# Softmax of a windowed attention: the maximum as a bias and the sum from ScalarE's accumulator, in eight calls per tile

## The chip, the cores and the metric

The kernel runs on one core of a Trainium2 chip. The metric is the device time of one execution in microseconds. The core has five engines with a queue of their own each: TensorE (PE: matmuls, with PEld for its weight loads), VectorE (DVE), ScalarE (ACT), GpSimd (POOL) and SyncE (SP), whose queue issues the DMAs here. An engine works through its queue in program order, and one engine waits for another by semaphores.

## The reference

Three stages follow one another, all in float32. First a chunked attention with 4 batches, 8 heads, 768 positions and a head size of 64: each chunk of 32 queries sees 8 memory keys, 16 keys to the left, its own 32 and 8 to the right, 64 keys in all.

```
scores = scale * matmul(q_c, k_full.T)
scores = scores - max(scores, axis=-1)
a = exp(scores)
a = a / (sum(a, axis=-1) + 1e-09)
out[chunk] = matmul(a, v_full)
```

Its output is laid out as 3072 tokens of 512 numbers. Then comes a gated layer, `(sigmoid(x @ w_gate) * (x @ w_val)) @ w_out` with 1536 inner columns, and a second layer, `silu(x @ w_in) @ w_out` with 2048 inner columns. Some weights come in as 8-byte floats.

## The kernel before, in words

**Attention tiles.** The attention is cut into 24 tiles of 128 tokens. A tile has, on each of the 128 partitions, eight groups of 64 scores: 512 columns, one PSUM bank. Four functions handle a tile, each a step of its own:
- `att_scores` (L181): 16 calls that write the scores into PSUM (L189), with masked columns at a sequence's ends (L197, L199), then on VectorE the maximum of each group (L202) and the subtraction that moves the scores to SBUF (L203), then on ScalarE one Exp over all 512 columns (L204).
- `att_norm` (L207): VectorE's sum of each group (L210), an addition of 1e-9 (L211), the reciprocal (L212) and the multiplication (L213).
- `att_turn` (L215): four transposes on TensorE (L219) and ScalarE's copy out of PSUM (L220).
- `att_pv` (L223): the product with v (L229) and VectorE's transpose into the x tile (L236).

**Opening.** Tiles 0 to 3 run before anything else (the loop at L386): in each turn the scores of tile i, the turn of tile i-2, the norm of tile i-1 and the product of tile i-3. Idle matmuls (L375) stand between them. The x tile is then split into a high and a low part (`split`, L79: ScalarE casts the high part at L82, VectorE or GpSimd computes the low part at L85), which gives each product three matmuls.

**Phase 1.** Six blocks of 512 tokens follow, each with 12 steps f. A step has the gate product into one PSUM bank (`pg`, L263), ScalarE's Sigmoid of it (L273), the value product into another bank (`pv`, L263), VectorE's multiplication of the two (L277), the split of the result g, and the output product of the step before (`y`, L90 to L94). The banks of `pg` and `pv` come from a ring of two: the next step's `pg` waits for the Sigmoid, the next `pv` for L277.

During block 0 a `Feed` brings in the weights. Each of its 36 units is loaded, scaled by ScalarE (`rebias`, L107), put together by three VectorE instructions (`join`, L115, L118, L122), and split into high and low parts (L82 on ScalarE, L85 on GpSimd). During blocks 1 to 5 a generator (`prepare2`) does much the same with the second layer's weights, with sums of them (L478) and with splits that are written to DRAM (`coi`, `coo`).

**Order around the change.** The whole order is written by hand. The attention of tiles 4 to 23 is spread over blocks 0 to 4, four tiles per block, by a table of events, at three places per step f:

```
at = 3 * NF1 * bi + 3 + 24 * jj // max(n - 1, 1)
for d, what in ((0, "scores"), (2, "norm"), (4, "turn"), (6, "pv")):
```

At each place the events come first, and then a step of the `Feed` (block 0) or of the generator (two places in three of the later blocks). So in ScalarE's queue the Exp of a tile stands ahead of that step's casts and rebias, and of the cast of g or of the next Sigmoid. In VectorE's queue the softmax steps stand ahead of a join and of L277. Exp and Sigmoid need different activation tables on ScalarE, so a table load stands ahead of the Exp and another ahead of the next Sigmoid.

**Phase 2.** The second layer (pairs of inner columns, L658, and its output product, L771) uses no attention code.

Of the kernel before, what the change touches and what calls it, by code (L numbers as in the profile page):

```python
# [8 lines left out]
F32 = mybir.dt.float32  # L9
F32R = mybir.dt.float32r  # L10
I32 = mybir.dt.int32
AF = mybir.ActivationFunctionType
ALU = mybir.AluOpType
AX = mybir.AxisListType

P = 128
B, H, S, D = 4, 8, 768, 64
CH, LEFT, RIGHT, NMEM = 32, 16, 8, 8
WIN = NMEM + LEFT + CH + RIGHT
# [7 lines left out]
SCALE = 1.0 / float(D) ** 0.5  # L27
# [20 lines left out]
def moe_kernel(ctx: ExitStack, tc: tile.TileContext, qh, kh, vh, wg, wv, wo, w2i, w2o, out):  # L48
    nc = tc.nc
# [106 lines left out]
            self.n += 1  # L156


    q_t, k_t, v_t, e_t, at_t, x32 = {}, {}, {}, {}, {}, {}

    def att_load_qk(t, qb, kt):
        nc.sync.dma_start(out=qb.rearrange("p g u q -> p (g u q)"), in_=qh[t])
# [18 lines left out]
    def att_scores(t, ps_sc, e):  # L181
        sc = ps_sc(f"sc{t}")
        scv = sc.rearrange("p (c2 a k) -> p c2 a k", c2=2, a=4)
        qb, kt = q_t.pop(t), k_t.pop(t)
        for c2 in range(2):
            for a in range(4):
                for cp in range(2):
                    c = 2 * c2 + cp
                    nc.tensor.matmul(  # L189
                        scv[cp * 64 : cp * 64 + 64, c2, a],  # L190
                        qb[:, 4 * a + c].rearrange("p u q -> p (u q)"),
                        kt[:, a, c],
                        start=True,
                        stop=True,
                    )
        if t % TPB == 0:
            nc.vector.memset(scv[0:64, 0, :, NMEM : NMEM + LEFT], NEG)  # L197
        if t % TPB == TPB - 1:
            nc.vector.memset(scv[64:128, 1, :, WIN - RIGHT : WIN], NEG)  # L199
        s3 = sc.rearrange("p (g k) -> p g k", k=WIN)  # L200
        m = att.tile([P, 8, 1], F32, tag="m", name=f"m{t}", bufs=2)
        nc.vector.tensor_reduce(m, s3, axis=AX.X, op=ALU.max)  # L202
        nc.vector.tensor_tensor(out=e, in0=s3, in1=m.to_broadcast([P, 8, WIN]), op=ALU.subtract)  # L203
        nc.scalar.activation(out=e, in_=e, func=AF.Exp, scale=SCALE)  # L204
        e_t[t] = e

    def att_norm(t, eng=nc.vector):  # L207
        e = e_t[t]
        r = att.tile([P, 8, 1], F32, tag="r", name=f"r{t}", bufs=2)
        nc.vector.tensor_reduce(r, e, axis=AX.X, op=ALU.add)  # L210
        nc.vector.tensor_scalar_add(r, r, 1e-9)  # L211
        nc.vector.reciprocal(r, r)  # L212
        eng.tensor_tensor(out=e, in0=e, in1=r.to_broadcast([P, 8, WIN]), op=ALU.mult)  # L213
# [69 lines left out]
    with tc.manual_schedule():  # L283
# [5 lines left out]
        att = att_cm.__enter__()  # L289
# [96 lines left out]
        for i in range(n0 + 2):  # L386
            if i < n0:
                att_scores(i, ps_y, es[i])
                idle(NI)
            if 0 <= i - 2 < n0:  # L390
                at = hold[0].tile([P, 512], F32, tag="sg", name=f"at{i - 2}", bufs=3)
                att_turn(i - 2, ps_a, at.rearrange("p (a b q) -> p a b q", a=2, b=2))
                idle(NI if i < 4 else 0)
            if 0 <= i - 1 < n0:
                att_norm(i - 1, nc.gpsimd if i - 1 in NQ else nc.vector)
            if 0 <= i - 3:
                att_pv(i - 3, ps_y, x32[0], (i - 3) * P)
                idle(NI if i < 4 else 0)
            if i == 1:
                prefetch(n0)  # L400
            if i == 4:
                prefetch_v(n0)
            if i == n0:
                units[0].rebias()
                units[0].join()
            if i == n0 + 1:
                units[0].part()
                units[1].rebias()
# [10 lines left out]
        for bi in range(NB1 - 1):  # L419
            n = BLOCKS1[bi + 1] // P  # L420
            for jj in range(n):
                t = starts1[bi + 1] // P + jj
# [4 lines left out]
        def run_events(i):  # L427
            for what, t, bn, jj in events.get(i, []):
                if what == "scores":
                    att_scores(t, ps_a, e_tile(t))  # L430
                    prefetch(t + 1)
                elif what == "norm":
                    att_norm(t)
                elif what == "turn":
                    att_turn(t, ps_a, at_tile(t))
                else:
                    if bn not in x32:
                        x32[bn] = x32_tile(f"x32_{bn}")
                    att_pv(t, ps_a, x32[bn], jj * P)
                    prefetch_v(t + 1)  # L440
# [498 lines left out]
```

## Time and profile before

| | |
|---|---|
| time of the runs, median of 3 | 1166.77 us (1166.34 to 1167.43) |
| the profiled execution | 1165.85 us |
| its span in the profile | 1164.1 us |
| busy: TensorE | 1138.2 us (98%) |
| busy: VectorE | 695.6 us (60%) |
| busy: ScalarE | 487.4 us (42%) |
| busy: GpSimd | 124.5 us (11%) |
| data moved | 248.51 MB, 213 GB/s on average |

The span runs from the first to the last recorded instruction; the execution's time has 1.75 us more around it. Busy shares are averages over stages that differ: phase 1 with the attention lies in roughly the first 700 us, phase 2 behind it. In the rows further down, a line such as L204 is a line of the kernel, `out<-in` are the program's names for tiles, and a time in square brackets, or behind the bar, is the idle time of the engine just ahead of the instruction, with what ended it.

### The profile page before, as it was taken

Reading aid. Unit: us, or ns where it says so; the run is one execution under the profiler, and the core shown is the slowest. Engines: PE = TensorE matmul, PEld = TensorE weight load, DVE = VectorE, ACT = ScalarE, POOL = GpSimd, SP = SyncE. Lnnn points to the kernel's source line nnn. Section 1 sums busy time; section 2 is a strip of 40 time slices with the busy share of each in tenths; the row PEclk is TensorE's granted clock in tenths of the full one; section 3 lists DMA queues with packets and bytes.
Section 4 is the critical chain, followed back from the end, with each engine's and each line's share of the span. In section 5 each row is a group of like instructions: output and inputs, shape, how many; then the busy total and the mean of one; then the engine's idle time right before and its main releaser. Section 6 shows DMA issues by size and latency. Waiting matters only on the chain.

```text
span 1164.1 us, 16020 instructions
## 1 busy us (share of the span) xinstructions
PE 1138.2 (98%) x6319; PEld 927.7 (80%) x6319; DVE 695.6 (60%) x965; ACT 487.4 (42%) x708; POOL 124.5 (11%) x94
## 2 busy tenths in 40 slices
PE   8889999999999999999999999999999999999998
PEld 7667777888888888888887888888888888888887
DVE  7999965455555554554564534347944369634665
ACT  3555544334434433443343224445434454344442
POOL 2545530000000000000000001111001110011000
PEclk9999999999999999999999999999999999999999
DMA  9777767667656666766565356566655575655552
GB/s 314 244 238 246 242 218 238 208 206 227 224 194 212 219 227 194 242 213 203 199 205 211 120 188 199 190 239 237 228 199 192 205 282 215 227 193 203 208 204 86
DMA packets 79210, 248.51 MB, mean 213 GB/s; under 512 B 7584, under 2 KB 23968, under 8 KB 69920
## 3 DMA queue, kind: packets, MB, share of 16 engines
q1 hardware_dynamic: 79136, 247.49, 62.4%
q8 instruction: 50, 0.82, 0.3%
q14 instruction: 24, 0.20, 0.0%
HBM read 199.23 MB, written 48.23 MB: 213 GB/s over the span
## 4 chain that ended last, share of the span: by engine, by line
PE 83%; DVE 12%; DMA 3%; issue 1%; ACT 0%; SPq 0%; DVEq 0%; ACTq 0%
PE o L771 20%; PE c L658 20%; PE pv L263 13%; PE pg L263 13%; PE y L90 5%; PE y L92 5%; PE y L94 5%; PE sc L189 1%; PE px L229 1%; DVE t_wg L122 1%; DVE t_wo L122 1%; DVE t_wv L122 1%; DVE stg_wv L118 1%; DVE stg_wo L118 1%; DVE stg_wg L118 1%; DMA v<-in_vh_dram 1%
## 5 line engine op out<-in xcount | busy, mean ns | idle before, releaser
L658 PE MATMUL c<-xp,wr 128*128 128x512 f32 x1008 | 229.1, 389 | 0.0
L771 PE MATMUL o<-gf,wr 128*128 128x512 f32 x1008 | 229.0, 389 | 0.0
L263 PE MATMUL pv<-x,w 128*128 128x512 f32 x864 | 216.1, 400 | 13.0 <-DVE sg L277 11.4
L658 PEld LDWEIGHTS c<-xp,wr 128*128 128x128 f32 x1008 | 189.2, 188 | 39.3
L771 PEld LDWEIGHTS o<-gf,wr 128*128 128x128 f32 x1008 | 189.2, 188 | 39.3
L263 PE MATMUL pg<-x,w 128*128 128x512 f32 x864 | 210.6, 392 | 1.6 <-POOL x L85 0.9
L263 PEld LDWEIGHTS pv<-x,w 128*128 128x128 f32 x864 | 162.9, 191 | 51.9 <-issue 14.3
L263 PEld LDWEIGHTS pg<-x,w 128*128 128x128 f32 x864 | 160.4, 188 | 38.2 <-ACT x L82 1.5
L85 DVE TENSOR_TENSOR gf<-g,gf 128x1024 fp32r<-128x1024 f32 x84 | 103.8, 1239 | 49.9 <-ACT gf L82 49.6
L82 ACT CAST gf<-g 128x1024 fp32r<-128x1024 f32 x84 | 88.1, 1053 | 86.9 <-PE o L771 73.3
L678 POOL TENSOR_TENSOR s<-s,s 128x512 f32<-128x512 f32 x24 | 35.9, 1497 | 820.7 <-ACT s L677 820.7
L82 ACT CAST g<-sg 128x512 fp32r<-128x512 f32 x72 | 44.7, 621 | 156.8 <-DVE sg L277 156.8
L273 ACT ACTIVATE sg<-pg 128x512 f32<-128x512 f32 x72 | 42.9, 596 | 74.8 <-PE pg L263 61.7
L630 DVE TENSOR_TENSOR s<-c,s 128x512 f32<-128x512 f32 x48 | 33.2, 691 | 65.1 <-PE c L658 63.1
L90 PE MATMUL y<-g,wor 128*128 128x512 f32 x240 | 66.3, 397 | 0.6 <-DVE y L532 0.6
L85 DVE TENSOR_TENSOR g<-sg,g 128x512 fp32r<-128x512 f32 x60 | 41.5, 692 | 41.7 <-ACT g L82 41.7
L92 PE MATMUL y<-g,wor 128*128 128x512 f32 x240 | 64.3, 390 | 0.0
L94 PE MATMUL y<-g,wor 128*128 128x512 f32 x240 | 64.2, 389 | 0.0
L277 DVE TENSOR_TENSOR sg<-pv,sg 128x512 f32<-128x512 f32 x72 | 49.3, 684 | 21.3 <-PE pv L263 21.2
L633 DVE TENSOR_TENSOR g<-g,g 128x1024 f32<-128x1024 f32 x48 | 58.4, 1216 | 0.0
L636 ACT ACTIVATE g<-s 128x512 f32<-128x512 f32 x48 | 30.3, 632 | 54.1 <-DVE s L630 54.1
L92 PEld LDWEIGHTS y<-g,wor 128*128 128x128 f32 x240 | 45.1, 188 | 9.6
(120 smaller groups left out, 1127.3 us busy)
## 6 DMA issues: line engine op xcount, KB each, us to landing
wr<-w2o_d SPq DMA_DIRECT2D x42, 1024.0 KB, 4.8
wor<-wo_d SPq DMA_DIRECT2D x60, 512.0 KB, 4.7
wr<-w2i_d SPq DMA_DIRECT2D x24, 1024.0 KB, 5.0
wr<-w2i_d SPq DMA_DIRECT2D x24, 768.0 KB, 4.4
w2o_d<-coo SPq DMA_DIRECT2D x56, 256.0 KB, 2.8
w2i_d<-coi SPq DMA_DIRECT2D x24, 512.0 KB, 3.0
qA<-in_qh_dram SPq DMA_DIRECT2D x21, 512.0 KB, 4.9
k<-in_kh_dram SPq DMA_DIRECT2D x21, 512.0 KB, 5.5
```

What stands on the lines that cost most here:

```text
L82: nc.scalar.copy(hi, src)
L85: lo_eng.tensor_tensor(out=lo, in0=src, in1=hi.bitcast(F32), op=ALU.subtract)
L90: nc.tensor.matmul(o, w_hi, x_hi, start=first, stop=False)
L92: nc.tensor.matmul(o, w_hi, x_lo, start=False, stop=False)
L94: nc.tensor.matmul(o, w_lo, x_hi, start=False, stop=last)
L263: nc.tensor.matmul(o[:, :n], w[:, pw, kt * P : (kt + 1) * P], x[kt][:, px, :n], start=i == 0, stop=i == len(steps) - 1,)
L273: nc.scalar.activation(out=sg[:, :n], in_=psg[:, :n], func=AF.Sigmoid)
L277: nc.vector.tensor_tensor(out=sg[:, :n], in0=psv[:, :n], in1=sg[:, :n], op=ALU.mult)
L633: nc.vector.tensor_tensor(out=o, in0=a, in1=b_, op=ALU.subtract)
L658: nc.tensor.matmul(o, w[:, pw, i % 4, kt * P : (kt + 1) * P], X[i][:, px, kt], start=first and j == 0, stop=j == 5, skip_group_check=not f ...
L678: nc.gpsimd.tensor_tensor(out=s5, in0=s5, in1=s1, op=ALU.add)
L771: nc.tensor.matmul(c[at[i], dp], w[:, pw, pl, dp * P : (dp + 1) * P], f[:, px, pl], start=i in (A11, S1, S2) and pp == 0 and j == 0, stop= ...
```

## The change

`att_scores` no longer subtracts. The maxima are multiplied by -SCALE on VectorE (128 x 8 numbers), and ScalarE computes the Exp straight from PSUM in eight calls, one for each group of 64 columns. Each call takes the group's scaled maximum as its bias, one number per partition, and the sum of its outputs goes to a column of `r` by the accumulator output. `att_norm` takes `r` as it is and leaves the sum out. Nothing else is changed: no tile is bigger, and no DMA, no event and no order of the steps is another.

```diff
-    q_t, k_t, v_t, e_t, at_t, x32 = {}, {}, {}, {}, {}, {}
+    q_t, k_t, v_t, e_t, r_t, at_t, x32 = {}, {}, {}, {}, {}, {}, {}
...
         nc.vector.tensor_reduce(m, s3, axis=AX.X, op=ALU.max)
-        nc.vector.tensor_tensor(out=e, in0=s3, in1=m.to_broadcast([P, 8, WIN]), op=ALU.subtract)
-        nc.scalar.activation(out=e, in_=e, func=AF.Exp, scale=SCALE)
-        e_t[t] = e
+        nc.vector.tensor_scalar(out=m, in0=m, scalar1=-SCALE, scalar2=None, op0=ALU.mult)
+
+        r = att.tile([P, 8, 1], F32, tag="r", name=f"r{t}", bufs=2)
+        for g in range(8):
+            nc.scalar.activation(
+                out=e[:, g], in_=s3[:, g], func=AF.Exp, scale=SCALE, bias=m[:, g], accum_out=r[:, g]
+            )
+        e_t[t], r_t[t] = e, r
 
     def att_norm(t, eng=nc.vector):
-        e = e_t[t]
-        r = att.tile([P, 8, 1], F32, tag="r", name=f"r{t}", bufs=2)
-        nc.vector.tensor_reduce(r, e, axis=AX.X, op=ALU.add)
+        e, r = e_t[t], r_t.pop(t)
         nc.vector.tensor_scalar_add(r, r, 1e-9)
```

## Rows read from the trace of the kernel before

**Rows 1.** The page, parts 1 and 2: busy times, and 40 slices in tenths.

```profile
PE 1138.2 (98%) x6319; PEld 927.7 (80%) x6319; DVE 695.6 (60%) x965; ACT 487.4 (42%) x708; POOL 124.5 (11%) x94
...
PE   8889999999999999999999999999999999999998
...
DVE  7999965455555554554564534347944369634665
```

**Rows 2.** Busy time by stretch: PE, PEld, DVE, ACT, POOL, clock, DMA share, GB/s.

```profile
28.00:150.00 122.00, 106.97 (x627) 81.95 (x626) 114.50 (x140) 66.65 (x106) 65.60 (x44) 0.96 0.74 242
262.00:374.00 112.00, 112.00 (x715) 91.01 (x714) 62.57 (x113) 44.12 (x68) 0.00 (x0) 1.00 0.67 220
```

**Rows 3.** Chain that ended last, 0 to 160 us: start, us, what.

```profile
20.53 5.91 DMA stg_wv<-in_wv_dram
...
28.97 1.45 DVE stg_wv L115
...
156.11 1.61 DVE t_wo L122
```

**Rows 4.** Groups by line and shape: count | busy us, mean ns | idle before.

```profile
L82 ACT CAST g<-sg 128x512 fp32r<-128x512 f32 x72 | 44.7, 621 | 156.8 <-DVE sg L277 156.8
L273 ACT ACTIVATE sg<-pg 128x512 f32<-128x512 f32 x72 | 42.9, 596 | 74.8 <-PE pg L263 61.7 <-DMA yd<-y 9.6 <-DVE y L532 2.3
L203 DVE TENSOR_TENSOR e<-sc,m 128x512 f32<-128x512 f32 x21 | 14.5, 691 | 0.7
L210 DVE TENSOR_REDUCE r<-e 128x8 f32<-128x512 f32 x21 | 14.2, 677 | 0.0
L204 ACT ACTIVATE e<-e 128x512 f32<-128x512 f32 x21 | 13.3, 633 | 37.0 <-DVE e L203 36.9
L211 DVE TENSOR_SCALAR r<-r 128x8 f32<-128x8 f32 x24 | 4.1, 171 | 0.8
L82 ACT CAST coo<-fo 128x256 fp32r<-128x256 f32 x8 | 3.2, 404 | 19.6 <-DMA w2o_d<-coo 19.6
```

**Rows 5.** Timeline of the opening: start, us, engine, line [idle before].

```profile
7.88 0.69 DVE L202 TENSOR_REDUCE m<-sc 128x8 f32<-128x512 f32 x1
...
19.38 0.60 PE L219 MATMUL pt<-ident,e_w 128*128 128x128 f32 x4
...
19.91 1.08 PE L229 MATMUL px<-v,at 128*32 128x128 f32 x32
20.02 0.58 ACT L220 COPY at<-pt 128x512 f32<-128x512 f32 x1 [1.62 <-PE pt L219]
...
25.42 0.65 PE L229 MATMUL px<-v,at 128*32 128x128 f32 x16 [0.70 <-DMA v<-in_vh_dram]
...
26.12 0.72 DVE L236 STREAM_TRANSPOSE x<-px 128x512 f32<-128x512 f32 x1 [0.54 <-PE px L229]
...
27.04 2.17 ACT L82 CAST x<-x 128x512 fp32r<-128x512 f32 x4
```

**Rows 6.** Timeline of block 0 around tile 5.

```profile
75.34 1.28 ACT L204 ACT_TABLE_LOAD   x1
...
76.64 0.63 ACT L204 ACTIVATE e<-e 128x512 f32<-128x512 f32 x1
...
77.68 0.67 ACT L107 ACTIVATE stg_wv<-stg_wv 128x512 f32<-128x512 f32 x1
...
80.14 0.69 DVE L118 SCALAR_TENSOR_TENSOR stg_wv<-stg_wv 128x512 int32<-128x512 int32 x1
```

**Rows 7.** Timeline of block 2 around its third tile.

```profile
333.22 0.69 DVE L202 TENSOR_REDUCE m<-sc 128x8 f32<-128x512 f32 x1 [4.17 <-PE sc L189]
...
334.66 0.63 ACT L204 ACTIVATE e<-e 128x512 f32<-128x512 f32 x1 [3.36 <-DVE e L203]
...
335.20 0.65 ACT L107 ACTIVATE stg_w2o<-stg_w2o 128x512 f32<-128x512 f32 x1
...
337.22 0.68 DVE L277 TENSOR_TENSOR sg<-pv,sg 128x512 f32<-128x512 f32 x1
...
338.67 2.88 PE L263 MATMUL pv<-x,w 128*128 128x512 f32 x12
```

## The prediction

> **What bounds the kernel now.** I read the busy shares by slice first. TensorE is at 9 tenths nearly everywhere; only in the first three slices (29 us each) is it at 8, and there VectorE is at 7 to 9 [rows 1]. The table by stage sharpens this. From 28 to 150 us VectorE is busy 114.5 of 122 us and TensorE 107; from 262 to 374 us TensorE fills the whole stretch, while VectorE and ScalarE use 62.6 and 44.1 of 112 us [rows 2]. The chain of waits names the work: up to 26.4 us it ends in DMA, then it stays on VectorE (join steps, with the softmax steps of four tiles among them) from 28.97 to 157.7 us, and behind that TensorE's own work takes over, as the second stretch of the table already says [rows 2, 3]. So there are three regimes: an opening held by loads (tiles 0 to 3), block 0 held by VectorE (tiles 4 to 7), and blocks 1 to 4 held by TensorE (tiles 8 to 23, one every eight or so steps of the schedule).
>
> **What is removed and added.** Per tile VectorE loses the subtraction (0.69 us) and the sum (0.67), and gains a multiplication of 128x8, which is the operation and shape of L211 (0.17) [rows 4]: 1.19 us less. ScalarE loses one Exp of 512 columns (0.63) and gets eight of 64, with a bias per partition and an accumulated sum; call their time together X. No DMA and no table load is added: all eight calls use one function, and the order of functions on ScalarE stays.
>
> **X.** The trace has neither a 64-column call nor an accumulator. Casts of 512 and 256 columns take 621 and 404 ns, so 0.85 ns per column and a fixed 0.19 us; the Sigmoid out of PSUM takes 596 ns at 512 columns, so 0.22 us at 64 [rows 4]. If the sum costs nothing more, X is 8 x 0.22 = 1.75 us: the lower end. The upper end is a call as dear as the whole row of before, 8 x 0.632 = 5.06 us. I take one further fixed cost per call for bringing out the sum, since it has to wait until the last column is through: 0.22 + 0.19 = 0.41 us, X = 3.3 us. That is nearer to the low end because all the rows say that the columns, not the start, make up the 0.63.
>
> The Trainium skill, "ScalarE: Activation LUTs", section "What ACT_TABLE_LOAD costs", gives an ACTIVATE with a pointer bias as about 280 ns + 0.833 ns per column, with about 93 ns of overlap between neighbours, and no price for the accumulator; 333 - 93 = 240 ns makes X about 1.9 us, an estimate by which the sum below would be -4.8 us instead of +6.3. The 512-column Exp in this trace (632 ns) is nearer to that page's 612 without a pointer than to its 707 with one; a call with a pointer is in no run here yet.
>
> **Opening (tiles 0 to 3).** Now the x cast that starts block 0 waits until 27.04: the last attention product sits until a v load lands (25.42), then comes its transpose [rows 5]. After the change ScalarE has a chain of its own. The first maximum ends at 8.57, with the multiplication 8.8. ScalarE's program holds four groups of eight calls with one copy between (0.58): 9.4 + 4X. Behind the last group, in program order, come a copy (0.58), a product (1.08), four transposes (0.60), two products (2 x 1.08), the stream transpose (0.72) and the 0.2 us up to the cast [rows 5]; with 0.45 for the hand-overs, 5.8. The cast then starts at 15.2 + 4X: later than 27.04 once X is over 2.95. At 3.3 that is **+1.3 us**, and it goes straight into VectorE's chain, which has no idle time to absorb it. Below 2.95 the load still decides and nothing changes.
>
> **Block 0 (tiles 4 to 7).** VectorE sets the pace, so 4 x 1.19 = **-4.8 us** is real, unless ScalarE's queue makes VectorE wait. Behind the Exp in ScalarE's queue stand a cast and the rebias of the next weight unit, for which VectorE's L118 waits. For tile 5 the Exp starts at 76.64, right behind the table load, and the rebias ends at 78.36; VectorE needs it at 80.14, which is 79.65 with the subtraction gone [rows 6]. Eight calls shift the rebias by X - 0.63, so VectorE waits X - 1.92. In the other three tiles the Exp may start 0.5 us earlier than now, since it no longer waits for the subtraction; the same reckoning gives X - 2.37, X - 2.38 and X - 2.39. At 3.3 the four waits are 4 x 3.3 - 9.06 = 4.1 us: **net -0.7 us**. The sum, 2 steps later, is far from any wait and is a clear gain. A longer ScalarE queue also moves GpSimd's work about, which stays the same 65.6 us in this stage [rows 2]; I take that as neutral.
>
> **Blocks 1 to 4 (16 tiles).** TensorE sets the pace, so VectorE's saving is worth nothing here: cover is TensorE itself. The added ScalarE time is covered as long as the queue behind it keeps its slack. The tightest case: the Exp at 334.66, then the rebias at 335.20, VectorE's L118 and L122, and in VectorE's order L277, which frees the PSUM bank that the next value product needs. L277 ends at 337.90, the product starts at 338.67 [rows 7]: slack 0.77. The calls can start at 334.15, so everything behind shifts by X - 1.14, and TensorE waits X - 1.91. Going through all 16 tiles alike, six have thresholds under 3.3: 1.91, 1.95, 1.97, 2.5, 2.7 and 3.1; one has 3.9; in nine a cast that waits for a DMA, or some 4 us of slack, hides it. At 3.3 the six waits come to **+5.7 us**. The opening's and block 0's other engines (POOL, SP) get no new instruction.
>
> **Sum.** 1.3 - 0.7 + 5.7 = **+6.3 us**. The profiled execution took 1165.85 us (its span is 1164.1, with 1.75 outside); so 1172.2 by that execution. The median of the runs is 1166.77, 0.9 above it, and the forecast against it is **1173.1 us**. A difference of 0.2% is 2.3 us, about what a measurement can tell here; the sum leaves that band above X = 3.0 (+2.3) and below X = 2.5 (-2.2).
>
> **Rivals.**
> - *Cheap calls, ends faster.* The sum comes out with the call and X is 1.75 to 2.4. For it: ScalarE is busy only 42% [rows 1], and the fixed part of its rows is small. Against: eight results per tile must be written somewhere. Then no wait in block 0 is long (under X - 1.92), and VectorE's saving stays: 1166.8 - 4.8 = 1162.0 us. It decides below 0.31 us per call. Chance 0.20. (The Trainium skill's price for a call, 240 ns by the page quoted above, speaks for this one.)
> - *Overlap, ends even.* ScalarE's neighbours start about 0.1 us before the one ahead ends (the Exp at 334.66 lasts 0.63, the rebias behind it is at 335.20 [rows 7]). If a call's start hides in this way behind the read-out of the one ahead, a call costs 0.31, X = 2.5: -3.9 in block 0, +1.7 in blocks 1 to 4, 1164.6 us. Chance 0.15.
> - *ScalarE bounds the opening and the queues.* The read-out waits for the pipe to drain and costs more than another start, X = 3.9 to 5.06. At 4.5: opening +6.2, block 0 +4.1, blocks 1 to 4 +13.5: 1190.6 us; at 5.06 about 1199. Nothing in the trace excludes it; against it is only that it takes more than two fixed costs per call. Chance 0.20.
>
> **Chances.** The forecast's case (X from 3.0 to 3.9, 1169 to 1182 us) gets 0.45. Slower by over 0.2%: 0.45 + 0.20 = 0.65; within: 0.15; faster: 0.20. The range takes in the cheap end and most of the dear case: 1162 to 1190 us.
>
> **What would show each step.** The rows of ScalarE at the activation line, with their count (8 x 24) and a second kind of row if the read-out is an instruction of its own, give X at once. The x cast of the opening at 27.0 or about 28.4 shows the first step. In 28 to 157 us VectorE's idle time in front of L118, put down to ScalarE's rebias, shows the second (hardly any now). In 160 to 600 us TensorE's idle time before the value product, put down to L277, shows the third (hardly any now). The prediction is wrong if X is as forecast and these waits do not appear, or if they appear at tiles that I counted as covered.

## The result, and the profile after

The kernel after the change takes **1182.59 us** (median of three executions, 1180.92 to 1184.66), the kernel before 1166.55 in the same comparison: a ratio of 1.014, 95% interval 1.0116 to 1.0163. A fourth execution took 2299.6 us, at the full granted clock, and is left out as a slow one (the median with it would be 1183.62). The kernel is slower by 16 us, where 6.3 were forecast; the time lies in the range. The profiled execution took 1182.59 us, its span is 1180.8, so 16.7 us more than before. By stage, from marks that both traces have:

| stage | mark | before | after | change | forecast |
|---|---|---|---|---|---|
| opening | x cast of block 0 starts | 27.04 | 27.41 | +0.4 | +1.3 |
| block 0 | first to eleventh of its twelve `sg` products (L277, now L280) | 41.22 to 154.19 | 41.59 to 160.22 | +5.7 | -0.7 |
| blocks 1 to 4 | first copy of block 0's output `y` out of PSUM to that of block 4's (L530, now L533) | 171.52 to 609.29 | 177.62 to 625.83 | +10.4 | +5.7 |

The rest of the 16.7, about 0.3 us, lies between and behind these marks. With the first product of block 1 as the end of block 0 (170.22 before, 176.32 after) its change is the same, +5.7; in three runs further down the two differ, and there both are given. The page, parts 1 and 2, beside [rows 1]:

```profile
PE 1141.2 (97%) x6319; PEld 928.5 (79%) x6319; DVE 667.1 (56%) x941; ACT 529.6 (45%) x1068; POOL 124.2 (11%) x94
...
PE   8888899999999999999999999999999999999998
...
DVE  5888874455444444454454543437954368634565
```

VectorE did get work taken off: 28.5 us. Yet TensorE is at 8 in the first five slices now instead of three. The two stretches of [rows 2], with the same columns:

```profile
28.00:150.00 122.00, 102.22 (x597) 78.13 (x598) 104.91 (x129) 68.98 (x160) 61.84 (x41) 0.94 0.72 233
262.00:374.00 112.00, 110.21 (x705) 89.20 (x704) 53.46 (x102) 51.14 (x127) 0.00 (x0) 1.00 0.66 213
```

In block 0 VectorE, busy 114.5 of 122 us before, now stands idle for 17 us instead of 7.5. In block 2 TensorE, which filled all 112 us, lacks 1.8. The groups of the activation's line, now L207, show what stands in ScalarE's queue (count | busy us, mean ns | idle before):

```profile
L207 ACT ACTIVATE e<-sc,m 128x64 f32<-128x64 f32 x168 | 50.1, 324 | 0.3
...
L207 ACT ACTIVATION_READ_ACCUMULATOR e<-sc,m 128x1 f32 x168 | 36.5, 217 | 0.0
...
L207 ACT ACT_TABLE_LOAD x21 | 26.9, 1283 | 55.8 <-DVE m L203 55.8
```

Each call has a second instruction behind it that reads out the accumulator. And the 21 table loads, each 1283 ns as before, now wait for VectorE's multiplied maxima: 55.8 us of idle time ahead of them. Before, that wait (37 us) stood behind the load, ahead of the Exp [rows 4]. The view of this one line shows why (count, shortest, median and longest ns, first and last start in us):

```profile
L207 ACTq EVENT_SEMAPHORE  x24: 17/17/38, 9.0 to 596.2; - x24
...
L207 ACT ACT_TABLE_LOAD  x21: 1283/1283/1283, 9.1 to 596.3; - x21
```

In each tile a wait stands in ScalarE's queue as an instruction of its own, and the load stands behind it. In the kernel before the same view of the Exp (L204) has no such row: the Exp carries its one wait itself, and the load ahead of it waits for nothing of the tile. The timeline of block 0's first tile (start, us, what, idle time before):

```profile
45.75 0.54 DVE L203 TENSOR_SCALAR m<-m 128x8 f32<-128x8 f32 x1
...
46.37 1.28 ACT L207 ACT_TABLE_LOAD   x1 [1.88 <-DVE m L203]
...
47.66 0.31 ACT L207 ACTIVATE e<-sc,m 128x64 f32<-128x64 f32 x1
47.87 0.19 ACT L207 ACTIVATION_READ_ACCUMULATOR e<-sc,m 128x1 f32 x1
47.97 0.30 ACT L207 ACTIVATE e<-sc,m 128x64 f32<-128x64 f32 x1
48.13 0.42 DVE L115 TENSOR_SCALAR stg_wo<-stg_wo 128x512 int32<-128x512 int32 x1
...
49.99 0.65 ACT L82 CAST w<-t_wg 128x512 fp32r<-128x512 f32 x1
50.49 0.70 ACT L107 ACTIVATE stg_wo<-stg_wo 128x512 f32<-128x512 f32 x1
50.69 4.61 PE L266 MATMUL pg<-x,w 128*128 128x512 f32 x12 [2.55 <-ACT w L82]
50.72 1.30 POOL L85 TENSOR_TENSOR w<-t_wg,w 128x512 fp32r<-128x512 f32 x1 [4.46 <-ACT w L82]
...
51.23 1.34 DVE L118 SCALAR_TENSOR_TENSOR stg_wo<-stg_wo 128x512 int32<-128x512 int32 x1 [2.67 <-ACT stg_wo L107]
52.67 1.58 DVE L122 SCALAR_TENSOR_TENSOR t_wo<-stg_wo 128x512 int32<-128x512 int32 x1
```

From one call's start to the next it is 0.31 and then 0.29 us (47.66, 47.97, 48.26, and so on), so eight take 2.33 us (47.66 to 49.99), well under the 3.3 of the forecast; the recorded durations overlap, and adding them up (0.32 + 0.22 for each of eight) would give 4.3. But the load comes first: from its start to the end of the calls it is 3.62 us, and the rebias starts at 50.49 instead of 47.15. VectorE waits 2.67 us for it. In the other three tiles of block 0 the wait is 2.71, 2.08 and 2.70, in sum 10.2 us, where the trace of before has none. The chain of waits now goes through ScalarE at this place (start, us, what):

```profile
46.37 1.28 ACT L207
...
47.66 0.94 ACT e L207 x6
...
50.64 0.57 ACT stg_wo L107
...
51.23 1.35 DVE stg_wo L118
```

In blocks 1 to 4 the waits of TensorE, from 170 to 612 us (engine and line, for whom: us in total, times, longest):

```profile
PE pv L266 <- DVE sg L280: 8.0, 5, 2.2
PE pt L222 <- DVE e L216: 1.1, 1, 1.1
...
```

Before, the same view held 0.2 us in all. So 9.1 of the 10.4 us are seen as waits of TensorE, 8.0 of them at the place that the prediction named. The third tile of block 2, beside [rows 7]:

```profile
341.54 0.69 DVE L202 TENSOR_REDUCE m<-sc 128x8 f32<-128x512 f32 x1 [2.01 <-PE sc L189]
...
342.51 1.28 ACT L207 ACT_TABLE_LOAD   x1 [4.19 <-DVE m L203]
...
346.13 0.70 ACT L107 ACTIVATE stg_w2o<-stg_w2o 128x512 f32<-128x512 f32 x1
346.87 0.69 DVE L118 SCALAR_TENSOR_TENSOR stg_w2o<-stg_w2o 128x512 int32<-128x512 int32 x1 [4.10 <-ACT stg_w2o L107]
...
348.21 0.68 DVE L280 TENSOR_TENSOR sg<-pv,sg 128x512 f32<-128x512 f32 x1
...
348.94 3.02 PE L266 MATMUL pv<-x,w 128*128 128x512 f32 x12 [1.79 <-DVE sg L280]
```

The maximum ends at 342.23 and the rebias starts 3.90 us later; before it was 1.29 us. ScalarE stood idle for 4.19 us ahead of the load, long enough to have loaded the table three times over.

### The profile page after: what moved, and what is told of

The parts are those of the page before. It is cut to its first block, busy times and chain, and to the rows that moved or that the text cites. A ratio compares the mean times of both kernels' runs of the same rounds, so it can differ in the third digit from the quotient of the medians.

```text
span 1180.8 us, 16382 instructions
## 1 busy us (share of the span) xinstructions
PE 1141.2 (97%) x6319; PEld 928.5 (79%) x6319; DVE 667.1 (56%) x941; ACT 529.6 (45%) x1068; POOL 124.2 (11%) x94
## 4 chain that ended last, share of the span: by engine, by line
PE 74%; DVE 13%; ACT 6%; DMA 6%; issue 1%; SPq 0%; DVEq 0%; ACTq 0%
PE o L774 19%; PE c L661 19%; PE pv L266 12%; PE pg L266 10%; PE y L90 4%; PE y L92 4%; PE y L94 3%; ACT e L207 2%; DMA w2i_d<-coi 2%; DVE t_wo L122 1%; ACT L207 1%; PE px L232 1%; DVE t_wg L122 1%; PE sc L189 1%; DMA yd<-y 1%; DVE sg L280 1%
## 5 line engine op out<-in xcount | busy, mean ns | idle before, releaser
L280 DVE TENSOR_TENSOR sg<-pv,sg 128x512 f32<-128x512 f32 x72 | 49.3, 684 | 17.8 <-PE pv L266 17.7
L85 DVE TENSOR_TENSOR coi<-fi,coi 128x512 fp32r<-128x512 f32 (+1 forms) x32 | 19.9, 621 | 65.5 <-ACT coi L82 65.5
L85 DVE TENSOR_TENSOR coo<-fo,coo 128x512 fp32r<-128x512 f32 (+1 forms) x32 | 19.9, 622 | 61.9 <-ACT coo L82 61.9
```

The source lines that it names most:

```text
L85: lo_eng.tensor_tensor(out=lo, in0=src, in1=hi.bitcast(F32), op=ALU.subtract)
L280: nc.vector.tensor_tensor(out=sg[:, :n], in0=psv[:, :n], in1=sg[:, :n], op=ALU.mult)
```

## The experiments

The theory from these traces: the load of the Exp's table has become late, since the first call waits for two engines (scores by TensorE, maxima by VectorE), and the wait for VectorE is an instruction of its own ahead of the load; the eight calls add 2.33 us to the queue; and both make VectorE and TensorE wait where the prediction had said. The rivals: the calls and their read-outs alone, and a queue delay that costs more than the lateness itself. Changes by stage below are those of single profiled executions, by the marks above; two kernels that are alike in blocks 1 to 4 (eight calls with the early load, without and with the rebias first in block 0) differ there by 1.8 us, which says how finely these can be read.

### The table load made early again

Ahead of a tile's scores an Exp of one column of a constant asks for the table, and waits for nobody.

```diff
     def att_scores(t, ...):
...
+        early = att.tile([P, 1], F32, tag="early", name=f"early{t}", bufs=1)
+        nc.scalar.activation(out=early, in_=ident[:, 0:1], func=AF.Exp)
```

> The changed kernel with one more ScalarE instruction at the head of each tile's scores: an Exp of one column of a constant, which waits for nothing of the tile. The table load should then stand ahead of it and no longer wait for the maxima. Theory A (late table: the 1.28 us load now stands between the maxima and the first call, so ScalarE's queue is 1.28 + 2.33 = 3.6 us behind the maxima instead of 2.33): nearly all of the 17 us goes away, 1162 to 1168 us; waits of the value product for L280 back under 4 us in all. Theory B (the eight calls and eight read-outs themselves fill ScalarE's queue, table or not): 1176 to 1184 us, waits as in the changed kernel.

Measured: 1169.36 us, ratio 1.0026 (1.0016 to 1.0035); block 0 +0.6, blocks 1 to 4 +2.8. The same tile as above:

```profile
44.39 1.28 ACT L186 ACT_TABLE_LOAD   x1
...
45.68 0.20 ACT L186 ACTIVATE early<-ident 128x1 f32<-128x1 f32 x1
...
46.28 0.31 ACT L209 ACTIVATE e<-sc,m 128x64 f32<-128x64 f32 x1 [0.40 <-DVE m L205]
...
49.11 0.70 ACT L107 ACTIVATE stg_wo<-stg_wo 128x512 f32<-128x512 f32 x1
...
49.85 1.33 DVE L118 SCALAR_TENSOR_TENSOR stg_wo<-stg_wo 128x512 int32<-128x512 int32 x1 [1.40 <-ACT stg_wo L107]
```

The load runs while the scores are still being computed, the wait of 1.40 us is 1.27 shorter than 2.67, about one table load, and 13 of the 16 us are gone by adding an instruction. The time is 1.4 us above the range of theory A and far below that of theory B: the late load is the larger part of the loss. What is left is not nothing: four waits of 1.40, 1.42, 0.81 and 1.42 us (5.05) still stand in block 0.

### One call of 512 columns, with and without the early load

One maximum per partition for all eight groups takes the place of one per group, so that one Exp with one bias reads PSUM; VectorE sums as before. (The quotient is the same mathematically, save for the 1e-9; a group whose scores lie far below the partition's maximum loses digits.)

```diff
-        m = att.tile([P, 8, 1], F32, tag="m", name=f"m{t}", bufs=2)
-        nc.vector.tensor_reduce(m, s3, axis=AX.X, op=ALU.max)
+        m = att.tile([P, 1], F32, tag="m", name=f"m{t}", bufs=2)
+        nc.vector.tensor_reduce(m, sc, axis=AX.X, op=ALU.max)
         nc.vector.tensor_scalar(out=m, in0=m, scalar1=-SCALE, scalar2=None, op0=ALU.mult)
-        r = ...
-        for g in range(8): ...
+        nc.scalar.activation(out=e, in_=s3, func=AF.Exp, scale=SCALE, bias=m)
...
+        nc.vector.tensor_reduce(r, e, axis=AX.X, op=ALU.add)
```

> One maximum per partition over all 512 columns, one Exp of 512 columns out of PSUM with it as its bias, and the sum back on VectorE. (The softmax is the same in exact arithmetic, with another shift.) The table load still waits for the maximum. Theory A: the queue behind the Exp is later than in the kernel before by 0.17 + 1.28 - 0.69 = 0.8 us, under every threshold: 1163 to 1168 us. Theory B: one call, so the time of the kernel before or a little less, 1163 to 1167 us. Theory C (a table load behind the maximum costs by itself, some 0.6 us in each of 20 tiles, whatever the calls take): 1174 to 1180 us.

> The one-call kernel with the same early Exp of one column. Theories A and B: within 2 us of the one-call kernel, 1162 to 1167 us, since VectorE is spared 0.5 us per tile in block 0 (4 x 0.5 = 2 us less than before). Theory C: 8 us or more below the one-call kernel.

Measured: 1165.11 us (ratio 0.9991, 0.9982 to 0.9999) with the load late, 1163.84 (0.9979, 0.997 to 0.9988) with it early. A late load alone costs 1.3 us here; ahead of eight calls the same load costs 13. The two delays add up in one queue, and only what exceeds the slack is paid.

### The accumulator alone, the bias alone

The first of these keeps VectorE's subtraction, so that all eight calls read SBUF and wait for VectorE alone; the second keeps the bias and leaves the accumulator out, with VectorE's sum in its place.

```diff
-        nc.vector.tensor_scalar(out=m, in0=m, scalar1=-SCALE, scalar2=None, op0=ALU.mult)
+        nc.vector.tensor_tensor(out=e, in0=s3, in1=m.to_broadcast([P, 8, WIN]), op=ALU.subtract)
...
-                out=e[:, g], in_=s3[:, g], func=AF.Exp, scale=SCALE, bias=m[:, g], accum_out=r[:, g]
+                out=e[:, g], in_=e[:, g], func=AF.Exp, scale=SCALE, accum_out=r[:, g]
```

```diff
-                out=e[:, g], in_=s3[:, g], func=AF.Exp, scale=SCALE, bias=m[:, g], accum_out=r[:, g]
+                out=e[:, g], in_=s3[:, g], func=AF.Exp, scale=SCALE, bias=m[:, g]
...
+        nc.vector.tensor_reduce(r, e, axis=AX.X, op=ALU.add)
```

> Only the second half of the change: VectorE subtracts as before, and eight Exp calls of 64 columns from SBUF give the sums. The first call then waits for VectorE alone, and the table load should wait for nothing. Theory A: queue 2.33 + 0.5 us behind the maxima's multiplication would be, -2.7 us in block 0 for the sum, +1.8 of waits there and +3.4 in blocks 1 to 4: 1166 to 1173 us. Theory B: 1176 to 1184 us.

> The first half of the change: maxima as the bias of eight calls, no accumulator, the sum back on VectorE. The table load still waits for the maxima. Theory A: calls at 0.2 us each without a read-out, 1.6 us, queue 1.7 us later than in the kernel before: block 0 about +1, blocks 1 to 4 about +2 to 3, 1168 to 1171 us. If the read-outs alone were the cost: 1163 to 1166 us. If they cost nothing (a call and its read-out overlap wholly): within 3 us of the changed kernel, 1179 us or more.

Measured: 1168.32 us (1.0016, 1.0007 to 1.0024) with the accumulator alone, 1176.01 (1.0085, 1.0072 to 1.0099) with the bias alone. The second was a miss: 1168 to 1171 were expected, and it is block 0 (+4.1 for about +1) and blocks 1 to 4 (+6.1 for +2 to 3) alike. The tile in question, with the bias alone:

```profile
45.42 1.28 ACT L206 ACT_TABLE_LOAD   x1 [1.87 <-DVE m L203]
...
46.71 1.75 ACT L206 ACTIVATE e<-sc,m 128x64 f32<-128x64 f32 x8
...
48.30 0.66 ACT L82 CAST w<-t_wg 128x512 fp32r<-128x512 f32 x1
...
49.56 1.33 DVE L118 SCALAR_TENSOR_TENSOR stg_wo<-stg_wo 128x512 int32<-128x512 int32 x1 [1.96 <-ACT stg_wo L107]
```

Eight calls without the accumulator take 1.59 us (46.71 to 48.30), 0.20 each; so the read-out adds 0.09 to a call. The load is late here and early in the kernel with the accumulator alone, so it is not the accumulator that makes it late. What goes with it is the second engine among the operands: with the bias alone the activation's line has 24 waits as instructions of their own, with the accumulator alone 2, both in the opening. (Source in PSUM and bias were not changed one by one.) The accumulator-alone calls read SBUF and have no bias; they follow one another every 0.24 us, so that queue is also 0.4 us shorter. Why the miss: I had reckoned with the slack of the prediction, and the wait of 1.96 us is more than 1 us longer than that gives. The runs that follow bear on this.

### The weight unit's cast and rebias ahead of the calls

In block 0 the events run inside the step of the `Feed`, behind the cast and rebias and ahead of the join. First with eight calls and the early load, then with one call and the early load.

```diff
-                    run_events(it + i)
+                    if bi:
+                        run_events(it + i)
...
-                        feed1.step()
+                        feed1.step(lambda: run_events(it + i))
```

> The kernel with the early Exp, and in block 0 alone the events moved behind the step's cast and rebias (ahead of its join), so that the eight calls no longer stand in front of the rebias that VectorE needs next. Theory A (queue order: VectorE waits because the rebias stands behind the calls): the four waits of 0.8 to 1.4 us before L118 go away and the time falls by some 5 us, to 1163 to 1166 us. Theory D (the time is lost to GpSimd's work beside VectorE, whatever the order): the waits go away but the join steps grow as much, 1167 to 1170 us.

> The one-call kernel with the early Exp, and in block 0 the events behind the step's cast and rebias. Block 0 of the one-call kernel had hardly any wait left for a rebias (its queue is 0.5 us earlier than in the kernel before). If the order costs nothing by itself: within 1 us of the one-call kernel with the early Exp, 1162.5 to 1164.5 us. If the casts in front make the softmax late: 1165 to 1167 us.

Measured: 1165.46 us (0.9991, 0.9983 to 1.0), with block 0 at -3.2 instead of +0.6 (-2.6 instead of +0.4 up to the first product of block 1); and 1164.85 (0.9985, 0.9976 to 0.9994), with block 0 at -2.2 (-1.2), where the one-call kernel with the early load has -1.9 (-1.8). The second time lies between its two expectations, and its interval overlaps that of the kernel without this order: whether the order costs one call something stays open. With eight calls one wait of 0.47 us is left of the 5.05, and VectorE's saving appears. So the queue order, not the calls themselves, makes block 0 dear. The saving is smaller than the 4.8 us of the prediction even with the waits gone (3.2, or 3.7 with the last one). In this kernel the 128 x 8 multiplication by -SCALE took 0.55, 1.19, 1.11 and 0.55 us in block 0's four tiles, against 0.17 in block 2; GpSimd is busy for half of block 0 and not at all in block 2 [rows 2]. VectorE is not slowed there but held: in all runs together 38 of these 128 x 8 operations by a constant took over 0.25 us, and every one of them ended 0.03 us behind the end of a GpSimd instruction that was running when it started.

### The kernel before, with its queue delayed

Copies of a spare tile of 256 columns, used by nobody, stand behind the Exp of tiles 4 to 23: three, then eight. They follow one another every 0.44 us, and make the next cast late by 1.17 and 3.35 us in block 0's first tile, more than the 1.1 and 2.9 that were reckoned with.

```diff
         nc.scalar.activation(out=e, in_=e, func=AF.Exp, scale=SCALE)
+        if t >= 4:
+            for _ in range(3):
+                nc.scalar.copy(spare, spare)
```

> The kernel before with three in-place copies of 256 columns on ScalarE behind the Exp of tiles 4 to 23 (about 1.1 us more in ScalarE's queue), nothing else. By the thresholds of the prediction (1.7 us of slack in each tile of block 0, 0.74 to 0.77 in three tiles of blocks 1 to 4): +0 in block 0 and +1 behind it, 1167 to 1168.5 us. If the true slack in block 0 is about 1 us shorter, because a later cast also makes GpSimd start later and VectorE then reaches its wait sooner: +2 in block 0, 1169 to 1171 us.

> The same with eight copies (about 2.9 us). By the prediction's thresholds: +5 in block 0, +11 in blocks 1 to 4, 1181 to 1184 us. With 1 us less slack in block 0: +9 to 10 there, 1185 to 1189 us. If delays of ScalarE's queue are not what costs the time: under 1175 us.

Measured: 1168.52 us (1.002, 1.0011 to 1.0029) and 1198.52 (1.0275, 1.0261 to 1.0289); in block 0 +0.0 and +8.5, in blocks 1 to 4 +3.3 and +23.2. A delay without any of the change gives waits at the same places, so the delay is the cause. The second was a miss, by 10 us, in part because the copies took longer than reckoned. The trace of before has 1.73 us of slack in block 0's first tile (the rebias is over at 47.82, L118 starts at 49.55), and yet a delay of 1.17 us already gives a wait:

```profile
47.89 0.61 ACT L82 CAST w<-t_wg 128x512 fp32r<-128x512 f32 x1
47.99 0.42 DVE L115 TENSOR_SCALAR stg_wo<-stg_wo 128x512 int32<-128x512 int32 x1
...
48.58 1.30 POOL L85 TENSOR_TENSOR w<-t_wg,w 128x512 fp32r<-128x512 f32 x1 [2.62 <-ACT w L82]
...
49.11 1.32 DVE L118 SCALAR_TENSOR_TENSOR stg_wo<-stg_wo 128x512 int32<-128x512 int32 x1 [0.70 <-ACT stg_wo L107]
...
50.53 1.60 DVE L122 SCALAR_TENSOR_TENSOR t_wo<-stg_wo 128x512 int32<-128x512 int32 x1
```

The kernel before, same place:

```profile
47.32 1.84 POOL L85 TENSOR_TENSOR w<-t_wg,w 128x512 fp32r<-128x512 f32 x1 [1.43 <-ACT w L82]
...
47.92 1.53 DVE L115 TENSOR_SCALAR stg_wo<-stg_wo 128x512 int32<-128x512 int32 x1
...
49.55 1.59 DVE L118 SCALAR_TENSOR_TENSOR stg_wo<-stg_wo 128x512 int32<-128x512 int32 x1
```

The cast for which GpSimd's split waits stands in the same queue as the rebias. Before, the split started at 47.32 and ran beside L115, which took 1.53 us. With the cast late, the split starts at 48.58, L115 runs alone in 0.42 us, and VectorE is at L118 at 48.41 instead of 49.45: one microsecond earlier at a wait whose releaser is later. It then meets the split in L118 and L122, and L122 takes 1.60 instead of 0.69. The slack in the trace of before held 1.0 us here that were GpSimd's doing. Again VectorE is held until GpSimd is through: in all runs every L115 that took over 0.6 us (108 of them) ended 0.28 to 0.30 us behind the end of a GpSimd instruction.

A wait that comes about in this way need not cost anything. With three copies the four waits of block 0 sum up to 2.2 us, and block 0 is not longer than before (+0.0): between the marks VectorE was busy for 104.2 us instead of 106.0, so it had done its work sooner by nearly as much as it then waited. With eight copies the waits sum up to 10.9 us, 2.0 of which are won back in this way, and block 0 pays 8.5.

With eight copies TensorE's waits from 170 to 612 us are 15.2 us by the view shown above for the kernel after, and three times the twelve value products behind such a wait took 4.6 us instead of 3.0:

```profile
355.54 4.61 PE L266 MATMUL pv<-x,w 128*128 128x512 f32 x12 [2.49 <-DVE sg L280]
```

That is 4.8 us more, so 20 of the 23.2; the rest I can't point to. The table by stretch, with the columns of [rows 2], shows the clock that was granted there, a mix of the two levels of 1.2 and 2.4 GHz:

```profile
355.50:360.00 4.50, 4.46 (x13) 3.50 (x14) 3.69 (x9) 3.01 (x4) 0.00 (x0) 0.62 0.00 0
```

In block 0, where VectorE sets the pace, such places stand in both kernels: three groups of twelve products took 4.5 to 4.6 us before (at 33.52, 87.93 and 121.70; the granted clock is 0.64 from 87.9 to 92.6), and three after (at 33.89, 50.69 and 125.99; the second is in the timeline above, behind 2.55 us in which TensorE had nothing to do). Behind block 0 neither kernel has one: the value products at 414.56 of the kernel after, behind 2.17 us, took 3.03. So in TensorE's stages the change does not pay this price, and the eight copies pay it three times. The length of the wait alone does not tell when: with eight copies the products at 474.90, behind 1.92 us, took 4.63.

### The delay put behind the cast

To tell GpSimd's part from the delay itself: eight copies between the cast and the rebias, in tiles 4 to 7 only, so that the cast and the split stay on time.

```diff
         def step(self):
...
+            if late:
+                late.pop()
+                for _ in range(8):
+                    nc.scalar.copy(spare_t[0], spare_t[0])
```

> The kernel before with eight idle copies (3.0 us) on ScalarE in tiles 4 to 7 only, now behind the cast that GpSimd waits for and still ahead of the rebias that VectorE waits for. If in block 0 the slack is short because the late cast also moves GpSimd's splits (they then run beside VectorE's instructions behind the wait): GpSimd stays on time, VectorE comes to its wait as late as in the kernel before, the slack is 1.7 us and block 0 gets longer by 4 x 1.3 = 5 us, 1171 to 1172.5 us. If it makes no difference where the copies stand: 8 us as with the copies ahead of the cast, 1174 to 1176 us.

Measured: 1172.58 us (1.0052, 1.0038 to 1.0065), block 0 +7.0.

```profile
46.51 0.61 ACT L82 CAST w<-t_wg 128x512 fp32r<-128x512 f32 x1
47.02 3.46 ACT L156 COPY spare<-spare 128x256 f32<-128x256 f32 x8
...
47.19 1.84 POOL L85 TENSOR_TENSOR w<-t_wg,w 128x512 fp32r<-128x512 f32 x1 [1.43 <-ACT w L82]
...
47.79 1.53 DVE L115 TENSOR_SCALAR stg_wo<-stg_wo 128x512 int32<-128x512 int32 x1
...
51.07 0.69 DVE L118 SCALAR_TENSOR_TENSOR stg_wo<-stg_wo 128x512 int32<-128x512 int32 x1 [1.75 <-ACT stg_wo L107]
```

With the split on time L115 takes 1.53 us again, and the wait is 1.75 us (1.71 to 1.79 in the four tiles) instead of 2.28 to 2.88 with the same eight copies ahead of the cast. The slack is back: the copies put the rebias 3.38 us later here, and 3.38 - 1.73 = 1.65. The sum agrees: the four waits are 7.0 us, VectorE's busy time between the marks is that of before (106.0 us), and block 0 costs 7.0. The time is at the upper end of the first expectation, which had reckoned with copies of 3.0 us. What the late cast itself adds in block 0 is the difference to 8.5, 1.5 us; which part of it GpSimd, the gate product or the next cast has was not taken apart.

### A version by stage

Eight calls with the accumulator only in tiles 4 to 7, where VectorE sets the pace; one call and VectorE's sum in all others, where TensorE does (with one maximum per partition, as above); the early Exp everywhere, and in block 0 the rebias first.

```diff
+        if 4 <= t < 8:
+            ...  # eight calls, as in the change
+        else:
+            ...  # one call of 512 columns
```

> Each form where the stage can use it: eight calls with sums in tiles 4 to 7 (VectorE's stage, with the early Exp and with the events behind cast and rebias), one call and VectorE's sum in all other tiles. From the stages measured so far: -3 in block 0, 0 to -0.5 behind it, 0 in the opening: 1162.5 to 1164 us, the lowest or level with the one-call kernels. If the eight calls keep no gain even in block 0: 1166 us or more.

Measured: **1162.47 us, ratio 0.9967 (0.9955 to 0.998)** against before: block 0 -3.7 (-2.3 up to the first product of block 1), blocks 1 to 4 -0.7. It beats the kernels before and after. Against the simpler one-call kernel with the early load (0.9979, 0.997 to 0.9988) the intervals overlap. Its two stretches:

```profile
28.00:150.00 122.00, 108.51 (x665) 84.43 (x664) 113.69 (x139) 74.63 (x170) 67.80 (x45) 0.96 0.74 242
262.00:374.00 112.00, 112.00 (x720) 90.84 (x713) 59.48 (x112) 45.45 (x73) 0.00 (x0) 1.00 0.64 211
```

TensorE is full in block 2 again, and in block 0 VectorE stands idle for 8.3 us, where the change had left it idle for 17, while TensorE does 1.5 us more work in the stretch than before.

### What the queue delay costs

Third tile of block 2, in six kernels: time from the end of the maximum to the start of the rebias, beyond the 1.29 us of before; the wait of the value product there; and the change in blocks 1 to 4.

| kernel | shift, us | wait there | shift less wait | blocks 1 to 4 |
|---|---|---|---|---|
| three copies | 1.18 | 0.31 | 0.87 | +3.3 |
| eight calls, early load | 1.34 | 0.51 | 0.83 | +2.8 |
| accumulator alone | 1.40 | 0.52 | 0.88 | +1.4 |
| bias alone | 1.88 | 1.05 | 0.83 | +6.1 |
| the change | 2.61 | 1.79 | 0.82 | +10.4 |
| eight copies | 3.37 | 2.49 | 0.88 | +23.2 |

The slack that the prediction read there, 0.77 us [rows 7], holds over the whole range to about 0.1 us, whatever delays the queue. What remains of the stage is that more places fall out of cover as the shift grows.

## Why the prediction was wrong

**X.** Sized wrongly, in the safe direction: 2.33 us instead of 3.3. A call takes 0.20 and its read-out 0.09 us, not 0.22 and 0.19. At the measured X the prediction's own sum is about -3.2 us (0 in the opening, 0.4 - 4.8 in block 0, 1.2 in blocks 1 to 4). So a better X would have made the forecast worse: something else cost the time.

**"No DMA and no table load is added ... the order of functions on ScalarE stays": the step that failed.** The count is right (21 loads, before and after) and the conclusion was wrong. The load's place in time moved from ahead of VectorE's result to behind it, because the first call now waits for two engines, and the wait for VectorE stands as an instruction of its own ahead of the load. The calls could not start "0.5 us earlier than now"; the queue behind the maxima holds 1.28 + 2.33 = 3.61 us, more than with X = 3.3 and an early load. Of the 16.0 us, 13.2 go with the early Exp. I saw the table load in [rows 6] ahead of its Exp and did not ask what it waited for.

**The Trainium skill on the price of a call.** The bias-only run gives 0.20 us from call to call, the kernel after 0.29 with the read-out. The Trainium skill, "ScalarE: Activation LUTs", section "What ACT_TABLE_LOAD costs", gives 0.24 for 64 columns with a pointer bias, an estimate worked out in the prediction; the measurements decide, and it was nearer to them than my 0.41. Its 1.9 us for eight calls against 2.33 lack the read-out. The prediction's 707 ns for a call of 512 columns with a pointer, which no run had shown yet, can be set beside 689 ns in the one-call kernel. The sum it led to, -4.8 us, failed at the same step as mine.

**Opening.** Held as a threshold: below X = 2.95 "the load still decides". X is 2.33, and the cast starts at 27.41, where the other kernels have it from 26.25 to 27.75, with and without the calls.

**Block 0.** The place of the wait was right (L118 for ScalarE's rebias, which the prediction named as its sign), the size was not: 10.2 us in four waits instead of 4.1. With 3.61 in the place of X the prediction's thresholds give 4 x 3.61 - 9.06 = 5.4. Most of the other 4.8 us of waiting is the step "GpSimd ... I take that as neutral". From the start of the maximum VectorE reaches L118 1.27, 1.07, 1.01 and 1.25 us sooner than before, where the prediction had some 0.5: 2.6 us more waiting in the four tiles, since GpSimd's late split leaves the instructions ahead alone and meets L118 and L122 instead. And the small multiplication, which starts the queue, took 0.54, 1.18, 0.17 and 0.55 us instead of 0.17 each: 1.8 us. Of the saving of 4.8 us, 4.3 are left: between the marks VectorE was busy for 101.6 us instead of 106.0.

**Blocks 1 to 4.** The mechanism and its places held best: five of the six counted tiles wait (1.02 to 2.17 us, in sum 8.0), all for L280. With 3.61 the six thresholds give 1.7 + 1.7 + 1.6 + 1.1 + 0.9 + 0.5 = 7.5 us. One wait was not counted, that of the transposes at 191.08 for the normalised tile (1.09), so 9.1 of the 10.4 us are seen; the other 1.3 I can't point to (two profiles of like kernels differ by more).

**The rivals.** "Cheap calls" had its price met (X of 2.33 in 1.75 to 2.4, 0.29 us per call), though the sum comes out by a read-out of its own, and its conclusion failed, as the late table load took back more than the calls saved. "Overlap, ends even" was right that neighbours hide part of each other, and failed by the same load. "ScalarE bounds the opening and the queues" had the right outcome for the queues by the wrong cause, dear read-outs. That the kernel came out slower, and inside the stated range, is luck: with its measured X the prediction says faster, and the late load, which none of its cases had, made up for it.

## What to carry to other kernels

An instruction that takes operands from two engines needs two waits, and one of them may stand in the queue ahead of the table load: look at what the load waits for, and if it stands behind data, put a one-column call that depends on nothing ahead of it. Waits that are reckoned from a trace hold only while the other engines keep their times: where one late queue releases both the waiting engine and an engine that holds it up, the waiting engine arrives sooner and waits longer. Such a wait is no loss by itself; what is lost is read from the length of the stage. And the same operation may have two best forms in one kernel: work is taken off VectorE where VectorE sets the pace, and ScalarE's queue is kept short where TensorE does.

## What the runs showed of the hardware

- The accumulator's read-out is an instruction of its own behind each call, and hides most of itself: 0.19 to 0.25 us recorded in tile 0 and tiles 4 to 23, 0.09 added to the time from call to call (0.29 us with it, 0.20 without).
- A table load can be kept waiting for an operand of the call behind it, by a wait that stands ahead of it as an instruction of its own. The load took 1283 ns in every place; what varied was when it was allowed to start.
- The VectorE operations by a constant seen here are held until the GpSimd instruction beside them has ended: 128 x 8 numbers took at most 0.17 us alone and up to 1.25 us in block 0 (L214 at 117.47 of the kernel after, which ended at 118.72, 0.03 us behind the GpSimd split beside it), and L115 took 0.42 or up to 1.53 us.
